# Five changes at once to an attention-and-highway kernel: accumulator banks, load order, norms, priorities, and who transposes v

## The chip, the cores and the metric

One core of one Trainium2 chip. The metric is device time in microseconds (us) of one execution; before: 273.93 us, median of three runs (273.48 to 274.74). Each set of experiments ran beside the kernel before on the same chip.

## The reference, cut to what matters

```python
def _attn_ref(q, k, v, tau):                 # q, k, v: (4, 6336, 256) f32
    qn = q / (norm(q, axis=1) + 1e-6)        # norms over the 6336 rows
    kn = k / (norm(k, axis=1) + 1e-6)
    s = kn.transpose(0, 2, 1) @ qn / tau     # 256 x 256 per batch
    a = softmax(s)
    return v @ a
def _moe_ref(x, w_h, w_t, b_t):              # x: the result above, (25344, 256)
    H = np.maximum(x @ w_h, 0.0)
    T = 1.0 / (1.0 + np.exp(-(x @ w_t + b_t)))
    return T * H + (1.0 - T) * x
```

## The kernel before

Each batch has two stages. **Stage 1** reads all of q and k of the batch and accumulates three Gram matrices in PSUM: k with q, k with k and q with q (the last two only for the norms). A **chain** of small steps then makes the softmax matrix and folds the two weights into it. **Stage 2** runs over 25 pairs of row tiles of v: transpose v, three products named h, t and d (`d` is `x` in the plan), then two ScalarE and two VectorE operations per pair, then a store. Stage 1 of the next batch is interleaved with stage 2 of this one.

A tile is 128 rows; a chunk is 8 tiles, 1 MB as f32; a batch is six chunks and a tail of two tiles of 96 rows. q, k and v are cast to f16 by the loads, which GpSimd issues; SyncE (SP) issues the stores and the DMA transposes.

Nothing is scheduled by hand: the program lists tasks with a priority (the smaller number goes first), a list scheduler orders them, and that order is emitted.

```python
APART = 4        # chunks of a batch whose q norms ScalarE and GpSimd make, not TensorE
BY_DMA = 1       # in the last batch, v is transposed by DMA from this chunk on
PRIO = {"tr": (-3.47, -0.36), "ev": (3.23, 2.26), "h": (0.45, 0.69), ...}   # (body, tail)

# the first loads
for j in range(1, NJ - 1):
    plan_load("q", 0, j); plan_load("k", 0, j)
for nm in "qk":
    plan_load(nm, 0, NJ)                       # the tails
for part in range(4):                          # last chunk in quarters
    plan_load("q", 0, NJ - 1, 4, part); plan_load("k", 0, NJ - 1, 4, part)
plan_load("q", 1, 0); plan_load("k", 1, 0)
# ... then the weights, the bias, the first chunk of v

def stage1(b, s):                              # one tile of q and k
    if s == order_of(b)[0]:
        sg_t[b] = [new(f"sg{c}", [P, 512], f32, f"sg{c}_{b}") for c in range(2)]
    # ... for c in range(2): k with q, k with k, and
        if not apart(b, s // CH):
            nc.tensor.matmul(sg[c][:, C + P : C + 2 * P], qa[:, cs], qa[:, cs], ...)

def squares(b, j, half):                       # ScalarE, for the chunks apart
    nc.scalar.activation(out=sq, in_=qa, func=Act.Square)
# ... and sum_squares adds them up on GpSimd
```

Names in the profile's lines: `sg` is a bank of the Gram matrices, `mr` the softmax matrix with the weights folded in; `vtps` is v transposed by TensorE in PSUM, `vtsb` its copy in SBUF, `vT` v as a DMA transposed it; `o` is the finished pair. A DMA share is the packets' time over that of 16 engines; it can be above 1, since packets overlap.

PSUM has eight banks: `sg0`, `sg1`, `vt`, `t`, two of `h` and two of `d`. Before, both batch 0 and batch 1 accumulate in `sg0` and `sg1`.

Of the kernel before, what the change touches and what calls it, by code (L numbers as in the profile page):

```python
# [11 lines left out]
f32 = mybir.dt.float32  # L12
# [3 lines left out]
P = 128  # L16
CH = 8
# [1 line left out]
V_BUFS = 5  # L19
O_BUFS = 7  # L20
LAG = 5
UNTIL = 65
AHEAD = 15
BY_DMA = 1
MOVE = 150e3
APART = 4
V_AHEAD = -2

PRIO = {
    "tr": (-3.47, -0.36), "ev": (3.23, 2.26), "h": (0.45, 0.69), "bias": (3.3, -0.05),  # L30
    "t": (-0.22, 4.42), "relu": (-3.45, 3.58), "x": (-1.14, 3.11), "gate": (2.73, -4.04),
    "prod": (1.3, -1.18), "res": (4.05, 6.98), "s1": (1.48, 0.05), "sq": (6.77, 9.48),
}
POW = 0.75
HEAD = 6
TAIL = 63
EV = BIAS = ("ACT", "DVE")
ENDS = [17.5, 46, 64.5]


class Ring:
# [11 lines left out]
class Task:  # L53
# [6 lines left out]
    def __init__(self, eng, key, pitch, lat, deps, fn, take=(), drop=(), size=0, follows=()):  # L60
        self.eng, self.key, self.pitch, self.lat = eng, key, pitch, lat
        self.deps, self.fn, self.take, self.drop, self.size = deps, fn, take, drop, size
        self.follows = follows
        self.start = self.done = None
        self.soft = False
        self.held = {}
        self.serial = False

# [10 lines left out]
class Plan:  # L79
# [1 line left out]



    RATE = 426e3
    HEAD = 1.5
    LAG = 1.8
    LANES = 8
# [15 lines left out]
    def run(self):  # L103
# [12 lines left out]
            lst.sort(key=lambda x: (x.key, x.n), reverse=True)  # L116
        engines = list(dict.fromkeys(x.eng for x in self.tasks if not isinstance(x.eng, tuple)))
        avail = {e: [x for x in self.tasks if e in x.engines() and not x.left and not (x.size or x.serial)] for e in engines}
        free = dict.fromkeys(engines, 1.2)
        lanes, order, events = [], [], [0.0, 1.2]  # L120
        t, left = 0.0, len(self.tasks)
        eps = 1e-6

# [21 lines left out]
                        avail[e].append(u)  # L145

        def pick(e):
            quiet = e == "POOL" and held(self.sums_stop)
            best = min(
                (x for x in avail[e] if ready(x) and not (quiet and x.soft)),  # L150
                key=lambda x: (x.key, x.n), default=None,
            )
            lst = in_order.get(e)
            if best is None and lst and ready(lst[-1]) and not (e == "POOL" and held(self.loads_stop)):
                return lst[-1]
            return best

        def held(stops):
            return any(
                a.start is not None and (b.done is None or b.done > t + eps) for a, b in stops  # L160
            )

        while left or any(queues.values()):
            for e in engines:
                x = pick(e) if free[e] <= t + eps else None
                if x is None:
                    continue
                if x.size or x.serial:
                    in_order[e].pop()
                else:  # L170
                    for other in x.engines():
                        avail[other].remove(x)
                    if isinstance(x.eng, tuple):
                        x.settle(e)
                left -= 1
                x.start = t
                order.append(x)
                for g in x.take:
                    x.held[g] = len(self.rings[g].freed)
                    self.rings[g].freed.append(None)  # L180
                free[e] = t + x.pitch
                release(followers.get(x, ()), free[e])
                events.append(max(free[e], t + 2 * eps))
                if x.size:
                    queues[e].append([x, float(x.size), t + self.HEAD])
                    events.append(t + self.HEAD)
                    if e == "POOL":
                        x.lane = len(lanes)
                        lanes.append(1e9)
                else:  # L190
                    finish(x, t + x.lat)

            act = [qq for qq in queues.values() if qq and qq[0][2] <= t + eps]
            share = self.RATE / max(1, len(act))
            nxt = [x for x in events if x > t + eps] + [t + qq[0][1] / share for qq in act]
            assert nxt, "no task can start"
            nxt = min(nxt)
            for qq in act:
                qq[0][1] -= share * (nxt - t)
            t = nxt  # L200
            events = [x for x in events if x > t - eps]
            for qq in act:
                if qq[0][1] < 1.0:
                    x = qq.pop(0)[0]
                    finish(x, t + self.LAG)
                    if x.eng == "POOL":
                        lanes[x.lane] = t + self.LAG
        self.end = max(x.done for x in order)
# [4 lines left out]
def kernel(  # L213
# [68 lines left out]

    def load_w(w, m):
        nc.gpsimd.dma_start(
            out=wht[:, :, m * C : (m + 1) * C], in_=w.rearrange("(kt jl) m -> jl kt m", kt=2)
        )

    def load_b(u):
# [34 lines left out]

    ld = {}

    def plan_load(nm, b, j, parts=1, part=None):

        n = CH // parts
        for s in range(0, CH if j < NJ else 1, n) if part is None else [part * n]:
            size = P * n * C * 4 if j < NJ else TR * 2 * C * 4  # L330
            tag = nm if j < NJ else f"tail_{nm}"
            x = plan.add(
                "POOL", len(plan.tasks), 0.54, 0, [], lambda: load(nm, b, j, s, n),
                take=[tag] if s == 0 else [], size=size,
            )
            x.fn = lambda nm=nm, b=b, j=j, s=s, n=n: load(nm, b, j, s, n)
            ld.setdefault((nm, b, j), []).append(x)

    def loaded(nm, b, s):

        if s >= S:
            return [ld[(nm, b, NJ)][0]]
        xs = ld[(nm, b, s // CH)]
        return [xs[(s % CH) * len(xs) // CH]]

    def drops(nm, b, s):

# [7 lines left out]
    plan_load("k", 0, 0)  # L355
    consts = plan.add("POOL", len(plan.tasks), 0.6, 1.5, [], constants)
    consts.serial = True
    for j in range(1, NJ - 1):
        plan_load("q", 0, j)
        plan_load("k", 0, j)  # L360
    for nm in "qk":
        plan_load(nm, 0, NJ)
    for part in range(4):
        plan_load("q", 0, NJ - 1, 4, part)
        plan_load("k", 0, NJ - 1, 4, part)
    plan_load("q", 1, 0)
    plan_load("k", 1, 0)
    w_ld = [
        plan.add(
            "POOL", len(plan.tasks), 0.75, 0, [], lambda w=w, m=m: load_w(w, m), size=P * 2 * C * 4  # L370
        )
        for m, w in enumerate((moe_w_h, moe_w_t))
    ]
    b_ld = [
        plan.add("POOL", len(plan.tasks), 0.54, 0, [], lambda u=u: load_b(u), size=40000)
        for u in range(2)
    ]
    plan_load("v", 0, 0)


# [31 lines left out]

    def order_of(b):


        if b:
            return list(range(NS))
        return [*range(S - CH), *range(S, NS), *range(S - CH, S)]

    def stage1(b, s):  # L420



        if s == order_of(b)[0]:
            sg_t[b] = [new(f"sg{c}", [P, 512], f32, f"sg{c}_{b}") for c in range(2)]
        sg = sg_t[b]
        qa, ka = sub("q", b, s), sub("k", b, s)
        first, last = s == order_of(b)[0], s == order_of(b)[-1]
# [40 lines left out]
    def plan_squares(b):  # L469

        ends, x = {}, None
        for j in range(APART):
            key = slot_of((b - 1) * NS + CH * j) + PRIO["sq"][0]
            parts = [
                plan.add(
                    "ACT", key, 0.97, 1.07, loaded("q", b, CH * j + CH // 2 * n),
# [2 lines left out]
                for n in range(2)  # L479
            ]  # L480
            ends[j] = parts
            n0 = len(plan.tasks)
            y = plan.add(
                "POOL", key, 2.36, 2.45, parts, lambda j=j: sum_squares(b, j, 0), drop=[(parts[1], "sq")]
            )
# [3 lines left out]
                lambda j=j: sum_squares(b, j, 2), drop=[(parts[0], "sq")],  # L489
            )  # L490
            for z in plan.tasks[n0:]:
                z.soft = True
        def over_partitions():
            sums[b, "ps"] = ps = new("vt", [P, 2], f32, f"sumps{b}")
            for c in range(2):
# [18 lines left out]
        else:  # L514
            nc.vector.tensor_copy(out=out, in_=in_)  # L515

    def plan_chain(b, first, last, key, sums_of_q):

        st = {}
        step = [0]  # L520
# [78 lines left out]
            for c in range(2):  # L599
                nc.scalar.copy(out=st["gs"][:, c, :], in_=sg_t[b][c][:, 0:C])  # L600

        gs = act(copy_g, 0.58, 0.7, [dk], drop=[(first, "sg0"), (first, "sg1")])
        iq = dve(lambda: (recip(0), dcat()), 0.82, 0.92, [nq, dk])
        ik = dve(lambda: recip(2), 0.3, 0.36, [nk])

# [46 lines left out]
        def trans(c):  # L652
# [2 lines left out]
                st["et"] = small.tile([P, 2, C], f16, tag="et", name=f"et{b}")  # L655
            for jk in range(2):
                nc.tensor.transpose(  # L657
                    st["eps"][:, c, jk, :], st["e"][:, c, bass.ts(jk, P)], ident0
                )

        def evac_et(c, e):
# [250 lines left out]
    ready = {}  # L912

    def plan_stage1(b):
        x = first = None
        part_ends, sums_of_q = ({}, []) if not apart(b, 0) else plan_squares(b)
        for n, s in enumerate(order_of(b)):
            key = -100 + n if b == 0 else slot_of((b - 1) * NS + s) + PRIO["s1"][0]
            deps = loaded("q", b, s) + loaded("k", b, s) + ([x] if x else [])
            x = plan.add(  # L920
                "PE", key, 0.33 if apart(b, s // CH) else 0.44, 0.66, deps, lambda s=s: stage1(b, s),
                take=["sg0", "sg1"] if n == 0 else [],
                drop=([] if apart(b, s // CH) else drops("q", b, s)) + drops("k", b, s),
            )
            x.lat = x.pitch if n < NS - 1 else 0.66
            if apart(b, s // CH) and s % CH == CH - 1:
                plan.add("NONE", 0, 0, 0, [x] + part_ends[s // CH], None, drop=drops("q", b, s))
            first = first or x
        ready[b] = plan_chain(b, first, x, -50, [sums_of_q] if apart(b, 0) else [])
        if b == B - 1:  # L930
            ends_of["sg0"] = ends_of["sg1"] = [x]

# [5 lines left out]
        return loaded("v", b, 2 * i) + loaded("v", b, 2 * i + 1) + [consts]  # L938

    def pr(kind, g):  # L940
        return g + PRIO[kind][g > TAIL]

    def plan_stage2(b):
        for i in range(NP):
# [127 lines left out]
```

## Time and profile before

| | before |
|---|---|
| time, median | 273.93 us |
| profiled span | 271.6 us |
| TensorE: work / first matmul / end | 237.9 / 9.0 / 264.1 us |
| TensorE's holes: before 50 us / 50 to 210 / after 210 | 11.8 / 3.4 / 1.8 us |
| first main matmul (h or t of stage 2) | 48.5 us |
| TensorE's end to the last store's landing | 6.4 us |

"Work" is the sum over all matmuls of the median start-to-start time of their form (the three start-up bias matmuls at 216 ns and the tiny sums of norms at 30 ns); a hole is what a start-to-start time has beyond that, so a lowered clock counts as holes too. That includes the first 5 us: until 14.2 us, where the record of the clock begins, matmuls of 256 columns start 213 to 215 ns apart instead of 109, though the page's PEclk row reads 9 there. So about 2.6 of the 11.8 us (half of 5.2) are no wait for data. The lines of the profile stand in the prediction below.

### The profile page before, as it was taken

The page shows a single profiled execution, that of the slowest core. Times are in us where ns is not written, and L with a number is a line of the kernel's source. Part 1 is how long each engine was busy: PE and PEld are TensorE (multiplying, and loading weights), DVE is VectorE, ACT ScalarE, POOL GpSimd, SP SyncE. Part 2 cuts the span into 40 slices and gives each one's busy share as a digit, 9 for nine tenths or more (in the row PEclk, how much of TensorE's full clock was granted, in tenths as well). Part 3 has the DMA queues.
Part 4 walks back from the last instruction along what each step waited for, and adds up shares of the span by engine and source line. Part 5 has one row for each costly group of instructions (what it writes and reads, how often), then busy time and mean ns, then how long its engine had stood idle before and what let it go on. Part 6 is the DMA issues. An engine that isn't in the chain of part 4 may idle for free.

```text
span 271.6 us, 6265 instructions
## 1 busy us (share of the span) xinstructions
PE 247.0 (91%) x2447; PEld 218.6 (80%) x2447; DVE 177.8 (65%) x366; ACT 191.5 (71%) x361; POOL 115.3 (42%) x153
## 2 busy tenths in 40 slices
PE   0697859999999999999999999999999999999980
PEld 0596757798999988999999888999998778878870
DVE  1000033658757897778777886767766888999991
ACT  1000034868969888889897888887875989988970
POOL 7221668596691095566928167775002110000000
PEclk9999997999999999999999999999999999999996
DMA  6999999999999999999999999999999999999996
GB/s 109 212 216 214 199 208 214 214 213 215 215 211 215 212 214 219 284 233 279 289 277 255 257 289 233 270 255 275 268 288 272 330 320 316 203 345 279 283 417 241
DMA packets 28430, 68.29 MB, mean 251 GB/s; under 512 B 13168, under 2 KB 15856, under 8 KB 25456
## 3 DMA queue, kind: packets, MB, share of 16 engines
q0 software_dynamic: 13184, 39.20, 73.6%
q1 hardware_dynamic: 15216, 28.69, 30.5%
q8 instruction: 19, 0.31, 0.4%
q14 instruction: 11, 0.09, 0.1%
HBM read 78.38 MB, written 25.95 MB: 384 GB/s over the span
## 4 chain that ended last, share of the span: by engine, by line
PE 76%; DMA 13%; DVE 4%; ACT 2%; issue 2%; POOL 1%; DVEq 0%; ACTq 0%; POOLq 0%
PE d L778 15%; PE h L778 15%; PE t L778 15%; DMA k<-in_k_dram 13%; PE sg L432 12%; PE sg L433 6%; PE vtps L738 6%; PE sg L435 2%; PE ah L667 1%; DVE pp L839 1%; PE t L809 1%; DVE o L858 1%; ACT d L818 1%; ACT uu L832 1%; PE eps L657 1%
## 5 line engine op out<-in xcount | busy, mean ns | idle before, releaser
L778 PEld LDWEIGHTS <-vtsb 128*128 128x128 f16 (+1 forms) x948 | 90.0, 99 | 13.4 <-issue 3.0
L432 PE MATMUL sg<-q,k 128*128 128x256 f16 x384 | 85.7, 278 | 15.2 <-DMA k<-in_k_dram 15.1
L839 DVE SCALAR_TENSOR_TENSOR pp<-uu,d 128x512 f32<-128x512 f32 (+1 forms) x100 | 67.7, 683 | 25.0 <-PE d L778 14.8
L433 PE MATMUL sg<-k 128*128 128x128 f16 x384 | 78.8, 224 | 0.0
L832 ACT ACTIVATE uu<-t 128x512 f32<-128x512 f32 (+1 forms) x100 | 59.5, 599 | 18.6 <-PE t L778 17.2
L858 DVE SCALAR_TENSOR_TENSOR o<-h,pp 128x512 f32<-128x512 f32 x96 | 65.3, 687 | 1.9
L818 ACT ACTIVATE d<-h 128x512 f32<-128x512 f32 (+1 forms) x100 | 57.8, 585 | 5.3 <-PE h L778 4.0
L432 PEld LDWEIGHTS <-k 128*128 128x128 f16 x384 | 38.5, 100 | 18.6 <-DMA k<-in_k_dram 15.9
L450 ACT ACTIVATE sq<-q 128x1024 f32<-128x1024 f16 x24 | 25.0, 1052 | 36.0 <-DMA q<-in_q_dram 36.0
L778 PE MATMUL t<-mr,vtsb 128*128 128x256 f16 x316 | 47.2, 272 | 0.4 <-ACT t L513 0.3
L778 PE MATMUL d<-mr,vtsb 128*128 128x256 f16 x316 | 46.5, 272 | 0.3 <-ACT d L818 0.2
L778 PE MATMUL h<-mr,vtsb 128*128 128x256 f16 x316 | 46.5, 272 | 0.3 <-DVE ri L635 0.3
L435 PE MATMUL sg<-q 128*128 128x128 f16 x192 | 42.8, 223 | 0.0
L433 PEld LDWEIGHTS <-k 128*128 128x128 f16 x384 | 38.3, 100 | 1.5 <-issue 0.3
L456 POOL TENSOR_TENSOR sq<-sq,sq 128x1024 f32<-128x1024 f32 x12 | 28.4, 2368 | 22.3 <-ACT sq L450 22.3
L513 ACT COPY t<-bias_all 128x512 f32<-128x512 f32 (+1 forms) x61 | 36.1, 592 | 1.3
L738 PE MATMUL vtps<-ident,v 128*128 128x128 f32 x144 | 27.9, 275 | 0.5 <-DVE vtsb L515 0.5
L549 DVE SCALAR_TENSOR_TENSOR junk<-sg,ident 128x128 f32<-128x128 f32 x16 | 4.6, 288 | 36.1 <-PE sg L435 35.5
L778 PEld LDWEIGHTS <-vT 128*128 128x128 f16 x240 | 23.4, 98 | 4.5 <-issue 0.5
L311 POOL DMA_DIRECT2D v<-in_v_dram x24 | 13.3, 555 | 31.1 <-PE vtps L738 21.9
L515 DVE COPY vtsb<-vtps 128x256 f32<-128x256 f32 (+2 forms) x42 | 17.6, 419 | 10.0 <-PE vtps L738 9.9
L311 POOL DMA_DIRECT2D q<-in_q_dram x27 | 15.1, 558 | 16.0 <-DMA q<-in_q_dram 8.9
(77 smaller groups left out, 252.1 us busy)
## 6 DMA issues: line engine op xcount, KB each, us to landing
out_dram<-o SPq DMA_DIRECT2D x23, 1024.0 KB, 9.1
v<-in_v_dram POOLq DMA_DIRECT2D x24, 512.0 KB, 18.1
q<-in_q_dram POOLq DMA_DIRECT2D x23, 512.0 KB, 16.7
k<-in_k_dram POOLq DMA_DIRECT2D x23, 512.0 KB, 17.6
out_dram<-o SPq DMA_DIRECT2D x2, 512.0 KB, 6.3
out_dram<-ot SPq DMA_DIRECT2D x4, 192.0 KB, 5.8
q<-in_q_dram POOLq DMA_DIRECT2D x4, 128.0 KB, 8.6
k<-in_k_dram POOLq DMA_DIRECT2D x4, 128.0 KB, 6.6
```

Source lines behind the costliest of these rows:

```text
L311: nc.gpsimd.dma_start(out=t[:, s : s + n, :], in_=main_rows(src)[:, j * CH + s : j * CH + s + n, :])
L432: nc.tensor.matmul(sg[c][:, 0:C], kc, qa, start=first, stop=False)
L433: nc.tensor.matmul(sg[c][:, C : C + P], kc, kc, start=False, stop=False)
L435: nc.tensor.matmul(sg[c][:, C + P : C + 2 * P], qa[:, cs], qa[:, cs], start=False, stop=last)
L456: add(out=sq, in0=sq, in1=other)
L513: nc.scalar.copy(out=out, in_=in_)
L738: nc.tensor.transpose(ps[:, u, 0:nr], v.bitcast(f32), ident0[0:nr, 0:nr])
L778: nc.tensor.matmul(out[0:nr, u, :], vt[u][kt][:, 0:nr], mr[kt][:, col * C : (col + 1) * C], **flags(u, kt))
L818: nc.scalar.activation(out=d[0:nr, :, :], in_=ps_t["h", b, i][0:nr, :, :], func=Act.Relu, scale=0.5)
L832: nc.scalar.activation(out=uu[0:nr, :, :], in_=ps_t.pop(("t", b, i))[0:nr, :, :], func=Act.Tanh, scale=-0.5)
L839: nc.vector.scalar_tensor_tensor(out=pp[0:nr, :, :], in0=el.pop(("uu", b, i))[0:nr, :, :], scalar=1.0, in1=ps_t.pop(("d", b, i))[0:nr, :, ...
L858: nc.vector.scalar_tensor_tensor(out=ot, in0=ps_t.pop(("h", b, i))[0:nr, :, :], scalar=0.0, in1=el.pop(("pp", b, i))[0:nr, :, :], op0=AluO ...
```

## The change

Its intent: start the chain of batch 0 and stage 2 earlier, take work off TensorE in the body, take work off DMA at the end. The core of the diff:

```diff
-UNTIL = 65
-AHEAD = 15
-BY_DMA = 1
+UNTIL = 73
+AHEAD = 16
+BY_DMA = 3
-APART = 4
-V_AHEAD = -2
+APART = 5
+V_AHEAD = 2
 PRIO = {
-    "tr": (-3.47, -0.36), "ev": (3.23, 2.26), ...
+    "tr": (24.974, 16.445, 34.195, 63.304),
+    "ev": (74.59, 73.008, 67.512, 50.704), ...
-    for j in range(1, NJ - 1):
+    for j in range(1, NJ - 2):
         plan_load("q", 0, j)
         plan_load("k", 0, j)
+        if j == 2:
+            # the tails of q and k and the bias, here
-    for part in range(4): ...
-    plan_load("q", 1, 0)
-    plan_load("k", 1, 0)
+    for j, s, n in ((NJ - 2, 0, 4), (NJ - 2, 4, 4), (NJ - 1, 0, 4), (NJ - 1, 4, 2), (NJ - 1, 6, 2)):
+        plan_load("q", 0, j, s, n)
+        plan_load("k", 0, j, s, n)
+    for s in range(0, CH, CH // 2):
+        plan_load("q", 1, 0, s, CH // 2)
+        plan_load("k", 1, 0, s, CH // 2)
+    def sg_tag(b, c):
+        return f"sg{c}" if b else "h"
-            sg_t[b] = [new(f"sg{c}", ...) for c in range(2)]
+            sg_t[b] = [new(sg_tag(b, c), ...) for c in range(2)]
```

Cut: the same re-pairing of the rows of the weights and of the softmax matrix (a permutation of the contracted index, no work more or less), small constants of the scheduler's own model, and the passing of a batch number to the priorities.

## The prediction

> **What bounds the kernel now.** I read the page's slices first, then its queues, then a table of stretches, then the waits of TensorE in order of time. The four lines of slices that matter, and the two queues:
>
> ```profile
> PE   0697859999999999999999999999999999999980
> PEclk9999997999999999999999999999999999999996
> DMA  6999999999999999999999999999999999999996
> GB/s 109 212 216 214 199 208 214 214 213 215 215 211 215 212 214 219 284 233 279 289 277 255 257 289 233 270 255 275 268 288 272 330 320 316 203 345 279 283 417 241
> ...
> q0 software_dynamic: 13184, 39.20, 73.6%
> q1 hardware_dynamic: 15216, 28.69, 30.5%
> ```
>
> Two resources are full, not one. The DMA row is 9 in every slice but the ends, and the queues' shares add up to more than 100% of sixteen engines. The PE row is 9 from the seventh slice on. The same in figures, by stage (columns: stretch, length, busy us of PE, PEld, DVE, ACT, POOL, granted clock, DMA share, GB/s):
>
> ```profile
> 0.00:36.00 36.00, 23.85 (x282) 21.61 (x283) 0.89 (x6) 1.28 (x1) 15.52 (x33) 1.00 1.01 191
> 36.00:50.00 14.00, 10.46 (x84) 7.89 (x83) 5.30 (x25) 7.66 (x16) 10.35 (x14) 0.88 1.10 210
> 50.00:110.00 60.00, 59.79 (x604) 53.62 (x602) 45.40 (x93) 50.02 (x96) 34.91 (x44) 1.00 1.07 216
> 110.00:210.00 100.00, 99.62 (x1022) 90.51 (x1020) 75.63 (x157) 82.95 (x152) 52.34 (x59) 1.00 1.06 268
> 210.00:262.00 52.00, 51.17 (x449) 43.24 (x448) 46.84 (x83) 47.92 (x97) 2.15 (x4) 1.00 1.07 304
> 262.00:272.00 10.00, 2.11 (x19) 1.71 (x16) 3.75 (x6) 1.68 (x4) 0.00 (x0) 0.74 0.71 286
> ```
>
> To 36 us TensorE waits for q and k of batch 0; from 36 to 50 there is the softmax chain of batch 0, with a hole and a lowered clock; from 50 to 264 TensorE has no holes worth naming; in 210 to 262 VectorE (90%) and ScalarE (92%) are nearly full too. The holes, from TensorE's timeline:
>
> ```profile
> 24.48 0.28 PE L432 MATMUL sg<-q,k 128*128 128x256 f16 x1 [1.94 <-DMA k<-in_k_dram]
> 29.35 0.28 PE L432 MATMUL sg<-q,k 128*128 128x256 f16 x1 [1.15 <-DMA k<-in_k_dram]
> 40.53 0.28 PE L432 MATMUL sg<-q,k 128*128 128x256 f16 x1 [3.02 <-DMA k<-in_k_dram]
> ```
>
> Busy is not work here, so I took the start-to-start times of the matmuls: 109 ns for 256 columns, 55 to 58 ns for 128, 109 ns for a 128-column f32 transpose, 216 ns for 512. With these medians for every matmul the work is 237.9 us. TensorE starts at 9.2 us and ends at 264.1, so the holes sum to about 17 us: 6.2 before 36 us, 5.6 between 40 and 50, 5.2 after 50. After TensorE's end come two VectorE operations (to 265.9) and a last store that lands at 270.5.
>
> DMA has no hole at all: the last stores land at 262.8, 265.2, 267.6, 268.9, 270.1 and 270.5, that is a MB per 2.4 us, one behind the other. A load of 1 MB takes 2.45 us throughout (GpSimd's waits for a free lane in the first 20 us are spaced so). The kernel moves 104.3 MB in that unit, 244 us of DMA, and the rest is start-up, constants and the DMA transposes of v.
>
> **What the Trainium skill says.** "DMA: Bandwidth & Descriptors", section "Anatomy of one DMA — SWDGE (gpsimd) path", fits a DMA as 2.0 us plus bytes over 436 GB/s. That makes 2.4 us of each further MB in a full queue; the trace has 2.45, so it agrees, and loads of half or quarter size should not cost bandwidth (the eight quarter loads landed 0.61 to 0.73 us apart, mostly 0.61 to 0.64). The same page's "Latency and other measured facts" gives a DMA transpose 261 GB/s, or 2.0 us for a chunk of 512 KB. The trace differs: a chunk is 2048 packets of 256 B at a mean of 23.7 ns, over 16 engines 3.04 us. I use that. "TensorE: Matmul & The Clock Gate", section "Wait — 56ns, not 53.3ns?", gives columns over 2.4 GHz plus 2.5 ns; for 256 that is 109 ns, as measured. "What's actually happening" there says that an idle window halves the clock; the clock is 0.69 in 40 to 44 us after the hole of 3.0 us, so the trace agrees in direction.
>
> **The change, part by part.**
>
> *v by DMA from chunk four.* In batch 3 chunks 1 and 2 (8 pairs of row tiles) go back from DMA transposes to TensorE. DMA loses 2 x 2048 packets x 23.7 ns / 16 = 6.1 us of packet time. With transposes running the DMA share is 1.14 to 1.16 in places and 1.06 in pure loads, so I count 5.2 to 5.8 us of wall time; accounting for landings after 210 us would give up to 3.4 us a chunk, 6.8. TensorE gains 32 transposes of 128 columns at 56 ns, +1.8 us. ACT and DVE gain 8 copies out of PSUM of about 0.55 us, 4.4 us over both, 2.2 us each, in the stage where both are over 90% busy.
>
> *Five chunks of q norms off TensorE.* In three batches 8 tiles lose two matmuls of 128 columns: 48 x 55 ns = -2.6 us of TensorE. ACT gets 6 squarings of 1.05 us (+6.3 us on 191.5), GpSimd 3 x (2.37 + 1.28 + 1.36) = +15 us on 115.3. Neither is near its limit in batches 0 to 2, where this lies.
>
> *Batch 0 in the banks of h.* Before, stage 1 of batch 1 needs the two sg banks that batch 0 still holds until its Gram matrices are copied (about 40.6 us). After, it may start as soon as its data land. This is worth little alone: the data themselves landed only at 40.5 in the kernel before (the hole's releaser is a DMA of k, not ScalarE).
>
> *Loads of stage 1.* The bias load goes early, so three bias matmuls (1.3 us at the low clock) move out of the chain into the time when TensorE starves. Chunk 4 in halves and chunk 5 in a half and two quarters let TensorE keep up: before, the last k landed at 35.6 and stage 1 ended at 37.3; after, it should end near 36.8. The first chunk of batch 1 comes in halves, so its first four tiles run from about 38.2 rather than 40.5, inside the chain. Then the chain is: diagonal and powers 2.4 us, broadcast 0.65, scaling 0.75, exp 0.65, transposes, copies and folding 3, so about 44.3 instead of the 48.4 that it took when interrupted. But the first chunk of v lands at about 44.5 (44.35 before) and must be transposed and copied: main matmuls start at about 45.2 instead of 48.5, with the same eight tiles of batch 1 done. Gain 3.2 us of TensorE time.
>
> *Priorities, the v loads earlier.* These reorder; one 0.22 us bias matmul falls away in the tail. I give them no gain; they decide whether the rest comes through.
>
> The sum for TensorE: -3.2 (holes) - 2.6 + 1.8 - 0.2 = -4.2 us; for the added copies at the end, where ACT and DVE are full, I add 0.5 to 1. TensorE would end at about 260.6 instead of 264.1. After it: 1.8 us of VectorE, about 2.6 for an unhindered small store (an estimate from 2.0 us fixed and 0.4 to 0.5 for its bytes) and 1.1 to the end of the span: 266.0. DMA alone allows 271.6 - 5.5 = 266.1. Both limits fall together, so I add half a us to one for their friction: a span of 266.6 to 267. The timed median lies 2.3 us above the profiled span (273.9 against 271.6), which gives 269.0 us, or 1.8% less.
>
> **Rivals.** (1) *DMA stays the bound and only the transposes count.* For it: no idle DMA anywhere, the last stores queued. Then all TensorE savings are hidden and the time is 267.7 to 268.7, the floor. Against: the stores are held back on purpose (the first goes out at 108 us) and the last ones then depend on results that come only as fast as TensorE makes them. (2) *The last batch turns ACT/DVE bound.* For it: 92% and 90% busy in 210 to 262, and pairs there take 1.41 us where VectorE alone needs 2 x 0.69. Against: only the first third of that batch has the new copies. If the whole 2.2 us comes through, 270.5. (3) *The chain gains nothing*, because TensorE's queue is in order and a load lands later than assumed; the new clock dip is as deep. For it: the 3.0 us hole came from just such a matmul queued ahead of the chain. Then TensorE ends near 263.5 and the time is about 272. (4) *GpSimd's extra 15 us delays load issues or the powers of the norms.* For it: sums of 2.4 us are not interrupted. Against: loads are issued some 17 us ahead of landing. It would cost under 1 us per batch, 271.
>
> **Range and chances.** The best case is the DMA floor with the dearer transposes, 266.5; the worst that I find likely is rival 3 with some of 2 or 4, 272.3. Between, the centre lies within 0.6 us of the 2% line at 268.45, so faster by over 2% gets 0.38, within 2% 0.59, and slower 0.03, since no part adds more than the DMA time saved.
>
> **What would show it.** Right: 6528 DMA packets of 256 B where there are 10624 now; TensorE's first main matmul near 45 us, the hole before it with a DMA of v as its releaser; TensorE's end near 260.6; DMA row still 9 to the end. Wrong: DMA slices below 9 in the last quarter (then TensorE or ACT/DVE binds and rival 2 or 3 holds); a main matmul first at 48 us; holes over 2 us in total after 210 us; waits of the first q or k matmul on GpSimd. A time under 267 would mean that DMA had slack that I did not see, for instance a transpose that holds up ordinary traffic.

## The result, and the profile after

270.12 us, median of four runs (269.99 to 270.21), against 273.71 us for the kernel before in the same rounds: a ratio of 0.9866, 95% interval 0.9833 to 0.9899, so 1.3% less. A ratio here is the mean time of one kernel's runs over that of the other's of the same rounds, so not quite the ratio of the medians. It lies within the 2% band, and inside the predicted range, 1.1 us above the predicted value.

| | before | predicted (its sums) | after |
|---|---|---|---|
| profiled span, us | 271.6 | 266.6 to 267 | 268.3 |
| TensorE work, us | 237.9 | 236.9 | 237.0 |
| holes before 50 us | 11.8 | 8.6 | 9.6 |
| holes 50 to 210 us | 3.4 | 3.4 | 5.2 |
| holes after 210 us | 1.8 | 2.3 to 2.8 | 1.6 |
| first main matmul, us | 48.5 | 45.2 | 45.65 |
| TensorE's end, us | 264.1 | 260.6 | 262.6 |
| from there to the last landing, us | 6.4 | 4.4 | 4.7 |

The slices and queues of the changed kernel's page:

```profile
PE   0697977999999999999999999999999999999991
...
PEclk9999999999999999999999999999999999999998
DMA  6999999999999999999999999999999999999995
GB/s 107 215 211 208 206 206 202 212 213 214 214 213 212 213 214 255 247 263 269 275 286 258 267 267 254 249 236 281 287 280 239 284 214 304 379 399 165 351 423 232
...
q0 software_dynamic: 13472, 39.20, 75.0%
q1 hardware_dynamic: 11120, 27.64, 29.0%
```

TensorE's clock no longer drops at 40 us, and the PE row is as full as before. The DMA row still reads 9 to the last slice. The second queue lost 4096 packets (15216 to 11120), as it should, but its share went only from 30.5% of 271.6 us to 29.0% of 268.3. Its 256-byte packets, 6528 where there were 10624, took 30.7 ns on average instead of 23.7: the packet time of the transposes fell from 15.8 to 12.5 us over 16 engines, not by 6.1.

The table of stretches of the changed kernel, columns as in the prediction:

```profile
0.00:36.00 36.00, 25.28 (x293) 22.45 (x294) 0.89 (x6) 2.46 (x3) 15.96 (x34) 1.00 1.02 191
36.00:50.00 14.00, 10.76 (x93) 7.98 (x92) 8.44 (x29) 8.01 (x17) 11.10 (x15) 1.00 1.12 205
50.00:110.00 60.00, 59.40 (x588) 52.83 (x587) 44.37 (x95) 51.00 (x96) 39.13 (x46) 1.00 1.06 222
110.00:210.00 100.00, 98.80 (x995) 89.26 (x994) 77.28 (x163) 85.98 (x157) 63.93 (x70) 1.00 1.06 264
210.00:262.00 52.00, 51.58 (x466) 43.74 (x464) 48.14 (x83) 47.62 (x96) 1.57 (x3) 1.00 1.05 316
262.00:272.00 10.00, 0.60 (x4) 0.34 (x3) 2.51 (x4) 0.00 (x0) 0.00 (x0) 0.82 0.35 135
```

In the last row the DMA share is 0.35 where it was 0.71: the stores no longer queue behind TensorE's end. The final small store was issued at 265.9 us and landed 4.7 us later before; now it is issued at 264.6 and lands 2.7 us later. POOL is busier by 4.2 us in 50 to 110 and 11.6 us in 110 to 210, ScalarE by 1.0 and 3.0: the fifth chunk of norms. In 36 to 50 the clock is 1.00 instead of 0.88.

TensorE's holes at the start, from its timeline (start, duration, instruction, idle before it and what ended it):

```profile
25.49 0.28 PE L452 MATMUL sg<-q,k 128*128 128x256 f16 x1 [1.43 <-DMA k<-in_k_dram]
...
38.33 0.28 PE L452 MATMUL sg<-q,k 128*128 128x256 f16 x1 [1.43 <-DMA k<-in_k_dram]
...
40.85 0.28 PE L452 MATMUL sg<-q,k 128*128 128x256 f16 x1 [0.53 <-DMA k<-in_k_dram]
...
44.77 0.41 PE L760 MATMUL vtps<-ident,v 128*128 128x128 f32 x2 [0.63 <-DMA v<-in_v_dram]
...
45.65 0.61 PE L800 MATMUL h<-mr,vtsb 128*128 128x256 f16 x4 [0.46 <-ACT vtsb L533]
```

The hole of 3.0 us ahead of batch 1's first tile became one of 1.4 and one of 0.5, for two half loads, and the start of stage 2 now waits for v itself at 44.77.

### The profile page after: what moved, and what is told of

The parts are those of the page before. It is cut to its first block, busy times and chain, and to the rows that moved or that the text cites. A ratio compares the mean times of both kernels' runs of the same rounds, so it can differ in the third digit from the quotient of the medians.

```text
span 268.3 us, 6249 instructions
## 1 busy us (share of the span) xinstructions
PE 246.4 (92%) x2430; PEld 216.6 (81%) x2430; DVE 181.6 (68%) x377; ACT 195.1 (73%) x365; POOL 131.7 (49%) x167
## 3 DMA queue, kind: packets, MB, share of 16 engines
q1 hardware_dynamic: 11120, 27.64, 29.0%
## 4 chain that ended last, share of the span: by engine, by line
PE 76%; DMA 12%; ACT 5%; POOL 2%; issue 2%; DVE 2%; ACTq 0%; DVEq 0%; POOLq 0%
PE h L800 16%; PE t L800 16%; PE d L800 15%; PE sg L452 12%; DMA k<-in_k_dram 10%; PE sg L453 6%; PE vtps L760 5%; DMA v<-in_v_dram 2%; ACT uu L854 2%; PE sg L455 2%; PE t L831 1%; PE vtps L754 1%; PE ah L689 1%; POOL q L327 1%; ACT d L840 1%
## 5 line engine op out<-in xcount | busy, mean ns | idle before, releaser
L800 PEld LDWEIGHTS <-vtsb 128*128 128x128 f16 (+1 forms) x1044 | 98.8, 99 | 17.3 <-issue 3.2
L453 PE MATMUL sg<-k 128*128 128x128 f16 x384 | 76.8, 223 | 0.0
L800 PE MATMUL t<-mr,vtsb 128*128 128x256 f16 (+1 forms) x348 | 52.2, 272 | 1.5 <-ACT t L533 1.2
L800 PE MATMUL h<-mr,vtsb 128*128 128x256 f16 (+1 forms) x348 | 51.2, 272 | 0.5 <-ACT vtsb L533 0.5
L800 PE MATMUL d<-mr,vtsb 128*128 128x256 f16 (+1 forms) x348 | 51.5, 272 | 0.1
L476 POOL TENSOR_TENSOR sq<-sq,sq 128x1024 f32<-128x1024 f32 x15 | 35.4, 2361 | 16.7 <-ACT sq L470 16.6
L455 PE MATMUL sg<-q 128*128 128x128 f16 x144 | 32.5, 226 | 0.0
L470 ACT ACTIVATE sq<-q 128x1024 f32<-128x1024 f16 x30 | 31.3, 1053 | 0.0
L535 DVE COPY vtsb<-vtps 128x256 f32<-128x256 f32 (+2 forms) x47 | 19.6, 418 | 7.0 <-PE vtps L760 6.7
L327 POOL DMA_DIRECT2D k<-in_k_dram x28 | 15.3, 548 | 13.1 <-DMA k<-in_k_dram 9.2
```

The source lines that it names most:

```text
L327: nc.gpsimd.dma_start(out=t[:, s : s + n, :], in_=main_rows(src)[:, j * CH + s : j * CH + s + n, :])
L453: nc.tensor.matmul(sg[c][:, C : C + P], kc, kc, start=False, stop=False)
L476: add(out=sq, in0=sq, in1=other)
L800: nc.tensor.matmul(out[0:nr, u, :], vt[u][kt][:, 0:nr], mr[kt][:, col * C : (col + 1) * C], **flags(u, kt))
```

## The experiments

Three sets of four. Setting APART back to 4 in the kernel after, or to 5 in the one before, can't be built: with the priorities of either the scheduler runs into buffers that wait for each other. So parts are undone in what is emitted rather than in the plan where that is possible. The first eight keep the emitted order of every engine but for what the text says, so what they show is not the scheduler's doing. The control of the last set is told first.

One source of scatter must be kept apart. In the profiles of the kernel before and its four variants the first main matmul starts at 48.5 to 50.6 us, before any of their edits acts: in the first 50 us the recorded clock is halved for 3.4 us in before and for 6.8 in each variant, and before's own runs spread likewise (mean clock 0.977 to 0.993). So the time from there to TensorE's end says more than the end itself; it is 215.6 us in before and 217.0 in after.

**The changed kernel again.** There is no edit.

> The changed kernel itself, as a control on the same chip as the three that follow: ratio to before about 0.986 as in its first rounds.

270.37 us, ratio 0.9873 (0.9832 to 0.9914). The first measurement repeats. The others are compared with 0.987.

### Does DMA bind the kernel before?

**Six stores of batch 0 halved, before:**

```diff
-                out=main_rows(ob)[:, j * CH + s : j * CH + s + n, :],
-                in_=og[(b, j)][:, s : s + n, :],
+                out=main_rows(ob)[:, j * CH + s : j * CH + s + (n if b else n // 2), :],
+                in_=og[(b, j)][:, s : s + (n if b else n // 2), :],
```

> The kernel before, its order of instructions kept, but the six chunk stores of batch 0 write half of their rows (wrong result on purpose): 3 MB less, 7.3 us less DMA. My theory: before is bound by DMA at its end, with TensorE some 2 us behind that limit, so it gets 1.5 to 2.5 us faster, and the last stores then follow TensorE's end without a queue. Rival 'DMA alone binds': 6 to 7 us faster. Rival 'TensorE alone binds': under 0.5 us.

275.32 us, ratio 1.0045 (0.9995 to 1.0095): nothing gained, so my theory missed. (The result is wrong, as meant.) Before's and this kernel's stretches, first before's and then two of this one:

```profile
200.00:210.00 10.00, 9.94 (x109) 9.06 (x108) 6.17 (x21) 6.45 (x14) 1.94 (x3) 1.00 1.05 283
```

```profile
200.00:210.00 10.00, 10.00 (x114) 9.33 (x112) 6.18 (x18) 6.15 (x12) 1.24 (x2) 1.00 0.52 146
210.00:262.00 52.00, 51.12 (x446) 42.95 (x444) 46.88 (x86) 47.90 (x98) 2.86 (x5) 1.00 1.07 291
```

The DMA share in 200 to 210 us fell from 1.05 to 0.52, so the 3 MB less really made room. But in 210 to 262 it is 1.07 again, and TensorE's end still has 6.9 us until the last landing. (From the first main matmul to TensorE's end it is 215.7 us, against 215.6 in before.) A spared transfer in the middle does not move the end: loads wait for buffers that computation frees, later stores wait for results. For the loads the trace shows it: GpSimd waits 15.7 us for TensorE's transposes to free a buffer of v, in before and in this run alike, and issues that load at 206.3 us here and at 205.1 in before: the room in 200 to 210 us draws no load forward. **A row of nines in the DMA line over the whole kernel is not the same as a kernel bound by its bytes.**

**The same in the kernel after** (same edit):

> The kernel after with the same 3 MB of stores left out (wrong result on purpose). My theory: after is bound by TensorE and the two VectorE operations behind it, DMA only just keeps up, so 0.3 to 1 us faster. Rival 'DMA still binds': 2 us or more.

269.79 us, ratio 0.9846 (0.9812 to 0.9881); the intervals overlap with after's. Nothing seen, as expected, but after the first miss this says little on its own.

**Six stores of batch 2 halved, before** (the edit above with `n // 2 if b == 2 else n`). These go out in the last stage:

> After the miss of before_half_stores: the kernel before, order kept, with the six chunk stores of batch 2 instead of batch 0 halved (wrong result on purpose). They go out after 210 us. Revised theory: DMA does not bind over the whole kernel (what is spared early is lost, since later stores and loads wait for results and free buffers), but in the last 60 us; so 1.5 to 3 us faster here, and TensorE's waits on transposed v vanish. Rival 'TensorE's order binds and the stores only trail': under 0.5 us.

271.54 us, ratio 0.9893 (0.9851 to 0.9936): 1.1% or 2.9 us less, by the same number of bytes that gave nothing earlier. Before's last stretch first, then two of this run:

```profile
262.00:274.00 12.00, 2.11 (x19) 1.71 (x16) 3.75 (x6) 1.68 (x4) 0.00 (x0) 0.72 0.59 238
```

```profile
210.00:262.00 52.00, 51.11 (x447) 43.17 (x446) 46.95 (x84) 47.97 (x99) 2.85 (x5) 1.00 1.02 267
262.00:274.00 12.00, 3.17 (x29) 2.68 (x26) 4.68 (x8) 2.75 (x6) 0.00 (x0) 0.82 0.38 148
```

The share in 210 to 262 is 1.02 instead of 1.07, and the last landing comes 3.9 us after TensorE's end instead of 6.4. TensorE itself was no quicker: 215.5 us from the first main matmul, and 2.0 us of holes after 210 us instead of 1.8, so the detail that its waits would vanish missed. So DMA does bind the end of the kernel before, by about 2.6 us, and through its last 60 us alone.

**The same edit in the kernel after:**

> The kernel after with the six chunk stores of batch 2 halved (wrong result on purpose). Theory: after is bound by TensorE to its end, so under 0.7 us faster than after. Rival 'DMA still binds in the last stage': 2 us or more faster.

269.91 us, ratio 0.9825 (0.9781 to 0.9870), a profiled span of 268.1 against 268.3 us. TensorE's end to the last landing: 4.1 us instead of 4.7. The final small store lands 2.1 us after its issue instead of 2.7, so after has 0.6 us of queue left at most. Relieving DMA's last stage brings this kernel 0.2 us in the profile (TensorE ended 0.3 us later in it); the ratio is 0.4% to 0.5% lower, inside the intervals. DMA has stopped being the bound.

### What is TensorE's time worth in each?

**Matmuls of the fifth chunk's q norms left out, before:**

```diff
-            if not apart(b, s // CH):
+            if not apart(b, s // CH) and not (b and s // CH == 4):
```

> The kernel before, order kept, but the 48 matmuls of q with q of the fifth chunk in batches 1 to 3 are left out (wrong result on purpose): 2.6 us less TensorE. My theory (DMA binds before): under 0.7 us faster, while TensorE's last matmul comes 2 to 2.6 us earlier. Rival 'TensorE binds': 2 to 2.6 us faster.

274.03 us, ratio 1.0003 (0.9971 to 1.0035). TensorE's work is 235.4 us, 2.5 less, and the time is the same: the part "five chunks of norms off TensorE", alone, is worth nothing in the kernel before. My detail was wrong: TensorE's end did not come 2 us earlier (264.7 us; 215.5 us from the first main matmul, where before has 215.6). In this profile the holes rose by 0.7, 0.8 and 1.5 us in the three stretches; one of 1.5 us at 251.7 is ahead of a matmul on DMA-transposed v. (The comparison with the reference still passed: one chunk of six missing in a norm is within its tolerance.)

**The same with batch 2's stores halved:**

> The same, and the 48 matmuls of q with q of the fifth chunk left out too (wrong result on purpose). Revised theory: with DMA's last stage relieved, the 2.4 us of TensorE that gave nothing alone now come through: 3.5 to 5.5 us faster than before. Rival: no more than before_half_b2 alone.

270.12 us, ratio 0.9837 (0.9780 to 0.9894): 0.6% below halved stores alone, with overlapping intervals. The direction fits, and the sum (1.6%, 4.5 us) is in the range that the theory gave; how much is TensorE's share stays loose. In the profile TensorE takes 213.8 us from its first main matmul, 1.7 less than with halved stores alone.

**The same matmuls put back, after:**

```diff
-            if not apart(b, s // CH):
+            if not apart(b, s // CH) or s // CH == 4:
```

> The kernel after, order kept, with the same 48 matmuls put back beside the squares (wrong result on purpose): 2.6 us more TensorE. My theory (TensorE binds after): 1.8 to 2.6 us slower. Rival 'DMA binds': under 0.7 us slower.

273.19 us, ratio 0.9976 (0.9937 to 1.0014): 1.1% or 3.0 us above after, and TensorE ends at 265.2 instead of 262.6 us, 219.6 instead of 217.0 us from its first main matmul. All of it comes through. The kernel after is bound by TensorE and by what follows its last pair.

### What is each other part worth, with the rest in place?

**Two more DMA transposes, after:**

```diff
+        if natural(b) and i in (4, 8):
+            extra = small.tile([P, CH, 2, P], f16, tag="extra", name=f"extra{i}")
+            src = tiles[("v", b, i // 4)][:, :, :].rearrange("p s c -> p (s c)")
+            nc.sync.dma_start(out=extra.rearrange("c s kt n -> c (s kt) n"), in_=src, transpose=True)
```

> The kernel after, with the chunks 1 and 2 of v of batch 3 transposed by DMA as well, into a buffer that nobody reads, beside TensorE's own transposes (right result): 6 us more DMA in the last stage and nothing else. Theory: DMA's last stage has only 1 to 2 us of slack, so 2.5 to 5 us slower than after; this is what the move of v alone is worth. Rival 'DMA transposes cost nothing on the way to the end': under 0.7 us.

275.41 us, ratio 1.0029 (0.9990 to 1.0069): 1.6% or 4.3 us above after, for two chunks. The stretch behind TensorE's end, after's first, then this kernel's:

```profile
262.00:274.00 12.00, 0.60 (x4) 0.34 (x3) 2.51 (x4) 0.00 (x0) 0.00 (x0) 0.85 0.29 113
```

```profile
262.00:274.00 12.00, 1.37 (x12) 0.92 (x9) 3.39 (x6) 1.01 (x2) 0.00 (x0) 0.69 0.80 317
```

The share behind 262 us is 0.80 instead of 0.29, and TensorE's end to the last landing takes 9.0 us instead of 4.7: the stores queue again. (TensorE ends 1.0 us later than in after, because the first v landed 1.1 us later in this profile, long before the transposes; from its first main matmul it takes 216.9 us.) Taking these two transposes off DMA is thus worth more than the whole change.

A rival stands: in the trace SyncE's DMAs go out one behind the other, and behind the two transposes the first four stores of the last batch's chunks go out 5.6 to 6.2 us later than in after (253.3 instead of 247.7 us for the first). The DMA share is 1.04 in 210 to 262 us and 0.95 in 262 to 272, with one dip to 0.78 in 248 to 252, so late issue left the engines little idle time, and the packets alone are 5.2 us more. That speaks for the packets, but no run issues the transposes from another queue.

**First chunk of batch 1 in one piece, after:**

```diff
         t = tiles[(nm, b, j)]
+        if nm != "v" and (b, j) == (1, 0):
+            if s:
+                return
+            n = CH
```

> The kernel after, order of the engines kept, but the first chunks of q and k of batch 1 are loaded in one piece each instead of two halves (right result). Theory: the three tiles of batch 1 that TensorE's queue holds ahead of the chain's broadcast then wait for k until 40.8 instead of 38.3 us, so the broadcast and the first main matmul come 2 to 2.5 us later (near 48), and the time is 1 to 2.5 us longer than after's. Rival 'the first chunk of v sets the start anyway': under 0.5 us longer.

272.63 us, ratio 0.9947 (0.9907 to 0.9986): 0.7% or 2.0 us above after's control. From TensorE's timeline:

```profile
40.73 0.28 PE L456 MATMUL sg<-q,k 128*128 128x256 f16 x1 [3.75 <-DMA k<-in_k_dram]
...
48.17 0.65 PE L804 MATMUL h<-mr,vtsb 128*128 128x256 f16 x4 [0.47 <-ACT vtsb L537]
```

One hole of 3.75 us until k lands, and the first main matmul is at 48.17 us, 2.6 later than the control's 45.57. The engine's queue is in order: the chain's broadcast stands behind three tiles of batch 1 and waits with them (it starts at 42.4 instead of 39.3 us). The lowered clock comes back with the hole, half speed for 3.4 us from 41.0 us, so the 2.6 us are the wait and the slow matmuls behind it together. Halving those two loads is what moves the start.

**Batch 0 back in the sg banks, after:**

```diff
-        return f"sg{c}" if b else "h"
+        return f"sg{c}"
```

> The kernel after with batch 0's Gram matrices back in their own two banks (right result; the plan moves the broadcast one tile of batch 1 earlier and changes nothing else of note). Theory, as predicted: the banks alone are worth little since the data of batch 1 land at the time at which the banks come free, so under 0.7 us longer than after. Rival 'the banks are what opens the chain': 2 us or more.

270.21 us, ratio 0.9861 (0.9825 to 0.9897): no difference from the control. From its timeline:

```profile
38.03 0.27 PE L452 MATMUL sg<-q,k 128*128 128x256 f16 x1 [1.37 <-ACT gs L620]
...
40.56 0.28 PE L452 MATMUL sg<-q,k 128*128 128x256 f16 x1 [0.22 <-DMA k<-in_k_dram]
```

Batch 1's first tile now waits for ScalarE's copy out of the bank rather than for k, and starts at 38.03 us, where k would let it start at much the same time (38.33 after). The part that names the change first is worth nothing on this chip at these load times.

**The old priorities, all else new:**

```diff
-PRIO = {"tr": (24.974, 16.445, 34.195, 63.304), ...}
+_P = {"tr": (-3.47, -0.36), ...}
+PRIO = {k: (v[0], v[0], v[0], v[1]) for k, v in _P.items()}
```

> All parts of the change, but the priorities of the kernel before (its two columns spread over the four; right result). The prediction gave the priorities no gain of their own. Theory: they decide the order in which TensorE, ScalarE and VectorE meet and which loads come first, so without them TensorE has several us more holes and the time is 3 to 8 us longer than after's, no better than before. Rival 'priorities are decoration': within 1 us of after.

278.84 us, ratio 1.0173 (1.0130 to 1.0217): 3.0% or 8.2 us above the control, and slower than before. The work is the same 237.0 us; the holes after 210 us are 10.2 us instead of 1.6. From TensorE's timeline:

```profile
260.22 0.60 PE L792 MATMUL h<-mr,vT 128*128 128x256 f16 x4 [1.14 <-DVE o L872]
...
264.36 0.60 PE L792 MATMUL h<-mr,vT 128*128 128x256 f16 x4 [1.14 <-DVE o L872]
...
268.49 0.60 PE L792 MATMUL h<-mr,vT 128*128 128x256 f16 x4 [1.14 <-DVE o L872]
```

Every 4.13 us, three pairs, a product h waits 1.1 us for the VectorE operation that frees a bank of h. The order in the tail was tuned for where these priorities put things; new parts need new ones. What the new priorities would have done for the kernel before, no run shows.

No experiment with a right result beats the kernel after. The one with the banks undone equals it and is simpler.

## Why the prediction was right or wrong

The time fell within the range and on the right side of 2%. By the prediction's own steps:

- **"Both limits fall together"**: right in the outcome, wrong in the reason for the DMA limit. The step "DMA alone allows 271.6 - 5.5 = 266.1" took DMA as one queue of bytes from end to end, since it had no hole. before_half_stores refutes it: 7.3 us less DMA in batch 0's stores gave nothing. before_half_b2 shows what holds instead: DMA binds only from about 210 us on. It held the end back by 2.6 us there (6.4 us behind TensorE instead of 3.9), where my first expectation said some 2 us. And in after it is TensorE that ends last, with 0.6 us of queue behind it.
- **"TensorE gains ... the sum -4.2 us"**: the work came as said (-0.9 us against -1.0). The holes did not. *Term one*, the start: predicted -3.2 us, measured -2.2. The first main matmul came at 45.65, not 45.2. The three reasons given for it were mostly one: the halves of q and k (after_q1_whole: 2.0 us of time, with the lowered clock that its hole brings back; the early bias load was not tested alone). *Term two*, "for the added copies at the end ... 0.5 to 1": the holes after 210 us did not grow, 1.8 to 1.6 us, so rival 2 is out. *A term that I did not have*: the holes between 50 and 210 us grew from 3.4 to 5.2 us. The largest are in the chain of batch 2, the kernel after's first, then the kernel before's:

```profile
153.61 0.60 PE L800 MATMUL t<-mr,vtsb 128*128 128x256 f16 x4 [0.28 <-ACT t L533]
...
155.58 0.60 PE L800 MATMUL t<-mr,vtsb 128*128 128x256 f16 x4 [0.65 <-ACT t L533]
```

```profile
156.06 0.60 PE L778 MATMUL t<-mr,vtsb 128*128 128x256 f16 x4 [0.33 <-ACT t L513]
```

Two waits for ScalarE's copy of the bias into the bank of t, where before had one. ScalarE is busier by 3.0 us in that stretch (the squarings). These make 0.8 us of the growth of 1.8. That this is the cause is argued, not shown: no run took the squarings alone away, and the priorities changed too.

- **"v by DMA from chunk four ... 5.2 to 5.8 us of wall time"**: the size holds for a transpose on the path (4.3 us for two chunks in after_more_tr, by 5.2 us of packet time), but against before the packet time fell only from 15.8 to 12.5 us, not by 6.1. The kernel before, with the same five transposed chunks, had only 2.6 us of queue to lose. In the new order the same 10624 packets take 26.7 ns each instead of 23.7, which is 2.0 us, and the last landing of after_more_tr is at 272.7 us, where before had it at 270.5. Why a packet takes longer there was not settled. The share of "1.14 to 1.16" with transposes running stands in no stretch that was asked for: the one 1.16 is in 40 to 44 us, before any transpose, and the last stage reads 1.06 to 1.09 up to 260 us. (Stretches of 4 us do reach 1.17.)
- **"This is worth little alone"**, of the banks: right; nothing could be measured.
- **"I give them no gain; they decide whether the rest comes through"**, of the priorities: right, and by more than I would have said: 8.2 us hang on them.
- **The tail after TensorE**: 4.4 us predicted, 4.7 measured, by two errors that nearly cancel: the unhindered last store takes 2.1 us (after_half_b2), not the estimated 2.6 (the fit behind that is one for the GpSimd path, and SyncE issues this store), and 0.6 us of queue was left.
- **"The timed median lies 2.3 us above the profiled span"**: this set the median of other runs against the profiled one, which itself was timed at 273.36 us, so 1.8 us above its span; after's was timed 1.9 above. The 0.5 us too much hid a part of the error in the span: 1.5 us there, 1.1 in the time. That is luck.
- **Readings**: the quarter loads landed 0.35 to 1.03 us apart, not 0.61 to 0.73 (their mean is 0.66), and TensorE's first matmul starts at 8.99 us, not 9.2. Neither carries the sum.
- **What would show it**: the packets (6528), the hole before the first main matmul with a DMA of v as its releaser, and a DMA row of 9 nearly to the end came as said; TensorE's end did not (262.6 instead of 260.6). The row of 9 was no sign of what binds: it stayed while TensorE bound the end.
- **Rival 3**, that the chain gains nothing because of an in-order queue behind a late load: it did not happen, but after_q1_whole produces it on demand. **Rival 4** on GpSimd: the powers and loads show no new wait on TensorE in the profile; no run tested it alone.

So the mechanism was right at the start, and at the end in that TensorE and DMA finish close together; the sum was 1.5 us too good in the span: 1.0 from the start, 1.8 from holes in the body and 0.3 from the tail, less 0.9 of copies at the end that cost nothing and 0.7 of friction that was added.

The parts, each undone with the rest in place, cost 4.3, 3.0, 2.0, 0 and 8.2 us. They add up to far more than the 3.6 us of the whole change. They are not shares: each is tuned around the others, and put into the old kernel alone a part can give nothing, as before_qq_out shows.

## What to carry to other kernels

An engine or queue that is busy from end to end is not yet a bound over its total: ask what of its work could be left out and whether the end would come sooner, and test that in the stage that ends last. Where two limits end within a few us of each other, relieve both, since either alone buys nothing or half. In an in-order queue, halve the load that stands ahead of the critical chain; and when parts of a tuned schedule move, its priorities must be tuned again before the change is judged.

## What the Trainium skill lacked or had wrong

- "DMA: Bandwidth & Descriptors", "Latency and other measured facts": 261 GB/s for a DMA transpose, so 2.0 us for 512 KB, an estimate from that figure. Here, with loads and stores beside it on the same engines, a chunk of 2048 packets took 3.0 us of packet time over 16 engines in the kernel before and 3.9 us after (30.7 ns a packet); two of them on the path cost 4.3 us.
- "Perfetto Trace Analysis", "Identifying the Most-Contended Engine", warns that occupancy misleads for DMA, and offers HBM utilization in its place. It has no word on a queue that is full because loads run ahead into free buffers: 384 GB/s over the whole span, and yet 3 MB less in the middle changed nothing, while 3 MB less in the last 60 us gave 2.9 us.
- "TensorE: Matmul & The Clock Gate", "What's actually happening": the clock falls after an idle window of about 3.4 us. Here shorter holes were enough: holes of 1.8 (after_old_prio), 2.2 (before_qq_out), 2.3 (before_half_b2) and 3.0 us (before) were each followed by half clock for 3.4 us, while others of 1.4 (after), 1.8 (after_half_stores), 1.9 (before) and 2.4 us (before_half_b2_qq_out) were not. The recorded stretches of full clock ahead of these drops are whole multiples of 3.41 us. Counted in steps of that length over all 14 profiles, up to TensorE's end, TensorE was idle for over 60% of eight steps, and half clock followed each; of four between 50% and 56% it followed one; below 50%, at full clock, none.
- No page says that the worth of a part must be measured with the rest of the schedule in place; here five parts undone singly cost 17.5 us in sum and all together brought 3.6.
